# Attention with a first expert woven in: step schedule, relu engine, transposition copy and far factors changed

## The chip, the cores and the metric

The kernel runs on one core of a Trainium2 chip. The metric is the device time of one execution in microseconds (us). The kernel before took 723.59 us, the median of 3 runs (722.73 to 723.69).

## The reference

Attention over 4 batches, 8 heads, 768 positions and head size 64, and then a mixture of 8 experts over the 3072 tokens. A flag for each head, an input of the launch, says whether the head has the full causal mask or keeps only 4 sink positions and a window of 64.

```python
scores = scale * np.matmul(q, k.transpose(0, 1, 3, 2))
scores = np.where(mask[None, :, :, :], scores, -1000000000.0)
a = np.exp(scores - np.max(scores, axis=-1, keepdims=True))
attn = np.matmul(a / (np.sum(a, axis=-1, keepdims=True) + 1e-09), v)
x = attn.transpose(0, 2, 1, 3).reshape(B * S, H * D)          # 3072 x 512
P = np.exp(x @ w_gate - (x @ w_gate).max())
for _ in range(8):
    P /= P.sum(1, keepdims=True) + 1e-09
    P /= P.sum(0, keepdims=True) + 1e-09
    P *= N / E
for e in range(E):                                             # 8 experts, 512 -> 1024 -> 512
    out += P[:, e:e + 1] * (np.maximum(x @ w1[e], 0.0) @ w2[e])
```

## The kernel before

**Attention.** Batch b, a group g of 256 queries and a half u of the heads (4 heads, two pairs a) are a unit; there are 24. For each pair the keys come in chunks, g + 1 of them: 512 score columns, or 384 for the last one. A (unit, pair, chunk) is a task, and two tasks are a round: 48 rounds, 12 for each batch, of which 2 belong to g = 0, 4 to g = 1 and 6 to g = 2. In a round n, in the order of the code (lines 575 to 586): score matmuls (line 444) into PSUM; exp on ScalarE (453); masks on VectorE (462, 465); the preparation of a later unit, which transposes keys and queries on TensorE (248) into one PSUM tile `tr` and copies them on VectorE, keys first, then queries (255); the turn of a finished unit, four transpositions (312) and a copy on ScalarE into xT (315); the products with v for the round before (283), normalized on VectorE (296, 297); and then steps of expert 0.

Blocks of keys far from the diagonal need no mask tile: for them v is multiplied by a factor of 0 or 1 for each head (and 1 in the sink rows) ahead of time, `emit_vfar`, lines 260 to 267. The factors `farf` have one value for each head and block kind, and the multiplication reads them broadcast along the head's 66 columns.

**Expert 0** fills TensorE during attention. A query group of 256 tokens gives four layer-1 steps (two blocks of 128 hidden units, 8 matmuls of 256 columns, line 351, relu from PSUM at line 356 or 358) which count 1 unit each, and two layer-2 steps (8 matmuls of 512 columns, line 365, copy on ScalarE at 369), which count 2. That is 96 units in all. 72 are spent in the rounds by `spend`, and 24 are kept for the Sinkhorn part (line 605), whose iterations are a chain of small VectorE operations with one matmul (607) each. `late` chooses the relu's engine: VectorE in all rounds, ScalarE after them.

The tiles of `tr`, `xt`, the steps and the logits share two PSUM slots (tag "mo").

**Order.** Up to round 5 the order on TensorE, VectorE and ScalarE is the order of the code (`manual_schedule`). From round 6 on the framework's planner orders each engine by its own model of times, with the code's order as priority: the trace has steps of expert 0 some rounds ahead of their place in the code, and the far products of g = 2 (emitted in round 6) at 24.88 us, before round 4's scores.

**After attention** come the experts 1 to 7 with a fast matrix scheme (lines 636 to 858), which keeps TensorE full.

The quota before: from round 4 on, each round spends the rest of the 72 units over the rest of the rounds, rounded up. So rounds 4 to 31 emit 2 units each and rounds 32 to 47 one.

Of the kernel before, what the change touches and what calls it, by code (L numbers as in the profile page):

```python
# [16 lines left out]
ts = bass.ts  # L17
# [19 lines left out]
def kernel(  # L37
# [170 lines left out]
    sinks = [rows for rows in sinks if rows.stop > rows.start]  # L208
    masks = [cp.tile([128, 2, 640], F16, tag=f"mask{j}", name=f"mask{j}") for j in range(4)]
    farf = cp.tile([128, H, 2], F16, tag="farf")  # L210

    def make_keep():
        nc.vector.scalar_tensor_tensor(
            out=keep[:, 256:512], in0=wm, scalar=1.0, in1=fm, op0=ALU.add, op1=ALU.mult)
        nc.vector.tensor_copy(out=keep[:, 0:256], in_=keep[:, 256:512])
        for rows in sinks:
            nc.vector.tensor_scalar(out=keep[rows, 0:256], in0=fm[rows, :], scalar1=2.0,
                                    scalar2=None, op0=ALU.mult)
        nc.vector.tensor_copy(out=keep[:, 512:640], in_=keep[:, 256:384])

    def make_masks(js):
        for h in [2 * j + hh for j in js for hh in range(2)]:
# [18 lines left out]
    def emit_prep(b, g, u):  # L241

        tr = psA.tile([128, 512], F32, tag="mo", bufs=2, name=f"tr_{b}_{g}_{u}").bitcast(F16)
        for i, src in enumerate(kq[b, g]):
            for a in range(2):
                for c in range(2):
                    for hh in range(2):
                        nc.tensor.transpose(
                            out=tr[64 * hh:64 * hh + 64, ts(4 * i + 2 * a + c, 128)],
                            in_=src[:, 4 * u + 2 * a + hh, c, :], identity=ident16,  # L250
                        )
        kTs[b, g, u] = ap.tile([128, 2, 256], F16, tag=f"kT{u}{g}", name=f"kT_{b}_{g}_{u}")
        qTs[b, g, u] = ap.tile([128, 2, 256], F16, tag="qT", bufs=3, name=f"qT_{b}_{g}_{u}")
        for i, dst in enumerate((kTs[b, g, u], qTs[b, g, u])):
            nc.vector.tensor_copy(
                out=dst.rearrange("r a (n c p) -> r a c n p", c=2, p=64),
                in_=tr[:, ts(i, 512)].rearrange("r (a c n p) -> r a c n p", a=2, c=2, p=64),
            )

    def emit_vfar(b, g):  # L260
        if b not in vfs:
            vfs[b] = ap.tile([128, H, 4, DV], F16, tag="vf", bufs=1, name=f"vf_{b}")
        for n in (2 * g - 2, 2 * g - 1):
            nc.vector.tensor_tensor(
                out=vfs[b][:, :, n, :], in0=vts[b][:, :, n, :],
                in1=farf[:, :, min(n, 1)].unsqueeze(2).broadcast_to([128, H, DV]), op=ALU.mult,
            )

    def keep_warm(lhsT, src, n):
        for _ in range(n):  # L270
# [33 lines left out]
    def turn():  # L304

        while turns:
            b, g, u = turns.pop(0)
            xn = xns.pop((b, g, u))
            xt = psA.tile([128, 512], F32, tag="mo", bufs=2, name=f"xt_{b}_{g}_{u}").bitcast(F16)
            for a in range(2):  # L310
                for sb in range(2):
                    nc.tensor.transpose(out=xt[:, ts(2 * a + sb, 128)], in_=xn[:, a, sb],
                                        identity=ident16)
            c0 = b * S + 256 * g
            nc.scalar.activation(
                out=xT[u][:, :, c0:c0 + 256], in_=xt[:, 0:512].rearrange("p (a c) -> p a c", a=2),
                func=AF.Copy, bias=0.0, scale=1.0)
            if u == 1:
                one, two = first_steps(b, g)
                at = 4 if (b, g) == (0, 1) else len(fillers)  # L320
                fillers[at:at] = one
                fillers.extend(two)
# [94 lines left out]
    def emit_scores(i, a, ci):  # L417
        b, g, u = units[i]
        if a == 0 and ci == 0:
            if u == 0:  # L420
                nb, ng = divmod(3 * b + g + 3, 3)
                if g:
                    emit_vfar(b, g)
                if nb < B:
                    load_kq(nb, ng)
                    if ng == 1:
                        load_v_heads(nb, 0, 4)
                        load_v_heads(nb, 4, 8)
                elif ng == 0:
                    expw[1] = load_expert(1)  # L430
            if i + 1 < len(units):
                preps.append(units[i + 1])
        if ci == 0:
            PTs[i, a] = ap.tile([128, 2, PTW], F16, tag="PT", bufs=4, name=f"PT_{b}_{g}_{u}_{a}")
        PT = PTs[i, a]
        qT = qTs[b, g, u]
        chunk = chunks_of(g)[ci]
        sc = psA.tile([128, 2, 512], F32, tag="sc", bufs=2, name=f"sc_{i}_{a}_{ci}")
        width = sum(c[2] for c in chunk)
        off = 0  # L440
        for kj, qlo, L in chunk:
            for hh in range(2):
                r0 = 64 * hh
                nc.tensor.matmul(
                    out=sc[:, hh, off:off + L],
                    lhsT=kTs[b, kj // 2, u][r0:r0 + 64, a, ts(kj % 2, 128)],
                    rhs=qT[r0:r0 + 64, a, qlo:qlo + L], start=True, stop=True,
                )
            off += L
        c0 = 512 * ci  # L450

        def exp():
            nc.scalar.activation(
                out=PT[:, :, c0:c0 + width], in_=sc[:, :, 0:width],
                func=AF.Exp, bias=0.0, scale=SCALE,
            )

        def mask():
            m = masks[2 * u + a]
            if ci == g - 1:  # L460
                d = PT[:, :, c0 + 256:c0 + 384]
                nc.vector.tensor_tensor(out=d, in0=d, in1=m[:, :, 384:512], op=ALU.mult)
            if ci == g:
                d = PT[:, :, c0:c0 + 384]
                nc.vector.tensor_tensor(
                    out=d, in0=d, in1=m[:, :, 0:384] if g == 0 else m[:, :, 256:640],
                    op=ALU.mult)
        return exp, mask
# [4 lines left out]
    def fill(n):  # L473

        while n > 0 and fillers:
            done = fillers.pop(0)()
            n -= done
            left[0] -= done

    def finish_sums(hold=False):  # L480
        held = []
        for (i, a), (gen, scale) in list(sums_of.items()):
            while run(gen, 1):
                pass
            del sums_of[i, a]
            held += scale
        if not hold:
            for f in held:
                f()
        return held  # L490


    rounds = len(tasks) // 2
    quotas = [0] * 4 + [1] * (rounds - 4)

    def spend(n):
        if quotas[n]:
            fill(-(quotas[n] * (24 - left[0]) // sum(quotas[n:])))

    def sum_later(n):  # L500
        for i, a, ci in tasks[2 * n:2 * n + 2]:
# [19 lines left out]
    with tc.manual_schedule(engines=engines):  # L521
        keep_warm(blank[:, 0:128], blank, 9)
        make_far()
        make_keep()
        round_first(0)
        emit_prep(*units[0])
        round_first(4)
        r0 = scores(0)
        soften(r0, (0,))
        warm(3)  # L530
        make_masks((0, 1))
        emit_prep(*preps.pop())
        warm(2)
        place_v(0)
        r1 = scores(1)
        soften(r0, (1,))
        soften(r1, (0,))
        sum_later(0)
        warm(6)
        make_masks((2, 3))  # L540
        soften(r1, (1,))
        scale = finish_sums(True)
        emit_prep(*preps.pop())
        for f in scale:
            f()
        warm(4)
        sum_later(1)
        r2 = scores(2)
        soften(r2, (0,))
        turn()  # L550
        scale = finish_sums(True)
        soften(r2, (1,))
        for f in scale:
            f()
        sum_later(2)
        emit_prep(*preps.pop())
        warm(2)
        soften(scores(3))
        place_v(1)
        turn()  # L560
        finish_sums()
        sum_later(3)
        warm(2)
        soften(scores(4))
        turn()
        finish_sums()
        sum_later(4)
        spend(4)
        soften(scores(5))
        turn()  # L570
        finish_sums()
        sum_later(5)
        spend(5)
        emit_prep(*preps.pop())
    for n in range(6, rounds):
        soften(scores(n))
        if n == 7:
            place_v(2)
        if preps:
            emit_prep(*preps.pop())  # L580
        turn()
        finish_sums()
        sum_later(n)
        if n % 12 == 2 and n > 12:
            emit_logits(n // 12 - 1)
        spend(n)
# [307 lines left out]
```

The softmax here doesn't subtract the row's maximum and nothing guards it: scores larger than these inputs give would overflow.

## Time and profile before

| | |
|---|---|
| median of 3 runs | 723.59 us |
| the profiled execution | 722.74 us, its span 721.00 us |
| attention's first score matmul, round 6, first Sinkhorn reduction | 8.76, 34.05, 170.52 us |
| experts 1 to 7 begin on TensorE | 195.51 us |
| busy in the span | PE 693.6, weight loads 573.7, DVE 578.8, ACT 412.9, POOL 151.3 us |
| line 358, relu on VectorE | 36 of 0.68 us |
| line 356, relu on ScalarE | 12 of 0.60 us |
| line 255, copies of keys and queries | 48 of 0.42 us |
| line 264, far products | 16 of 0.69 us |

Engines: PE is TensorE, DVE VectorE, ACT ScalarE, POOL GpSimd. PE's busy time takes in its pipeline, so a busy PE is not one at its peak; the distances between the starts of matmuls tell more: 0.109 us for 256 columns and 0.216 us for 512 where nothing is in the way. A row of a table by stage has the stretch, its length, then busy time and number of instructions of each engine, the granted clock of TensorE as a share, the share of the DMA engines and GB/s. In a timeline a row has the start, the duration, engine, line, operation, tiles written and read, shapes, and in brackets the idle time of the engine before it and what ended that.

### The profile page before, as it was taken

The page shows a single profiled execution, that of the slowest core. Times are in us where ns is not written, and L with a number is a line of the kernel's source. Part 1 is how long each engine was busy: PE and PEld are TensorE (multiplying, and loading weights), DVE is VectorE, ACT ScalarE, POOL GpSimd, SP SyncE. Part 2 cuts the span into 40 slices and gives each one's busy share as a digit, 9 for nine tenths or more (in the row PEclk, how much of TensorE's full clock was granted, in tenths as well). Part 3 has the DMA queues.
Part 4 walks back from the last instruction along what each step waited for, and adds up shares of the span by engine and source line. Part 5 has one row for each costly group of instructions (what it writes and reads, how often), then busy time and mean ns, then how long its engine had stood idle before and what let it go on. Part 6 is the DMA issues. An engine that isn't in the chain of part 4 may idle for free.

```text
span 721.0 us, 17111 instructions
## 1 busy us (share of the span) xinstructions
PE 693.6 (96%) x6944; PEld 573.7 (80%) x6944; DVE 578.8 (80%) x1193; ACT 412.9 (57%) x770; POOL 151.3 (21%) x183
## 2 busy tenths in 40 slices
PE   7899999998999999999999999999999999999995
PEld 3566665665678888888888888888888888888884
DVE  7748675764789997888789888988888788887887
ACT  4675656674497555555555555555555555555550
POOL 6403040000002122212121222123121312121210
PEclk9999999998999999999999999999999999999999
DMA  9999394000344349434953395439642964245774
GB/s 179 179 171 104 31 92 42 2 2 2 54 79 74 54 70 165 85 56 74 153 91 65 63 147 101 75 60 145 104 75 48 146 107 80 48 79 109 148 156 126
DMA packets 84224, 65.62 MB, mean 91 GB/s; under 512 B 48304, under 2 KB 64688, under 8 KB 84144
## 3 DMA queue, kind: packets, MB, share of 16 engines
q0 software_dynamic: 74976, 57.17, 56.8%
q1 hardware_dynamic: 7536, 6.30, 3.7%
q8 instruction: 54, 0.88, 0.5%
q10 hardware_dynamic: 1632, 1.05, 0.5%
q14 instruction: 26, 0.21, 0.1%
HBM read 52.45 MB, written 6.29 MB: 81 GB/s over the span
## 4 chain that ended last, share of the span: by engine, by line
PE 68%; DVE 1%; issue 0%; ACT 0%; DVEq 0%
PE l1y L709 19%; PE l2y L778 19%; PE l2w L778 10%; PE l1w L709 10%; PE l2z L778 5%; PE l1z L709 5%; DVE acc_84 L795 1%; DVE S_7_5_10710 L646 0%; DVE S_7_5_10713 L646 0%; DVE S_7_5_10712 L646 0%; DVE acc_83 L795 0%; ACT R_3772 L718 0%; DVEq L889 0%; ACT add L792 0%; DVE S_7_5_10711 L646 0%
## 5 line engine op out<-in xcount | busy, mean ns | idle before, releaser
L792 ACT ACTIVATE add<-l2w,Pne 128x256 f32<-128x256 f32 x80 | 33.6, 473 | 66.1 <-PE l2w L778 64.2
L351 PEld LDWEIGHTS <-w_0_125 128*128 128x128 f16 x384 | 37.4, 102 | 8.7 <-issue 3.0
L792 ACT ACTIVATE add<-l2y,Pne 128x256 f32<-128x256 f32 x80 | 33.8, 474 | 10.9 <-PE l2y L778 10.2
L792 ACT ACTIVATE add<-l2z,Pne 128x256 f32<-128x256 f32 x80 | 33.6, 472 | 8.7 <-PE l2z L778 8.7
L800 POOL DMA_DIRECT2D acc_79<-add x21 | 17.7, 844 | 78.8 <-ACT add L792 57.7
L800 POOL DMA_DIRECT2D acc_82<-add x21 | 17.8, 847 | 68.0 <-ACT add L792 68.0
L800 POOL DMA_DIRECT2D acc_80<-add x21 | 17.7, 845 | 67.9 <-ACT add L792 67.9
L800 POOL DMA_DIRECT2D acc_81<-add x21 | 17.7, 844 | 68.0 <-ACT add L792 68.0
L800 POOL DMA_DIRECT2D acc_83<-add x18 | 15.1, 840 | 54.7 <-ACT add L792 46.8
L800 POOL DMA_DIRECT2D acc_84<-add x18 | 15.4, 854 | 44.2 <-ACT add L792 43.7
L795 DVE SCALAR_TENSOR_TENSOR acc_79<-l2y,Pne,acc_79 128x256 f32<-128x256 f32 x42 | 18.3, 476 | 7.2 <-PE l2y L778 7.1
L795 DVE SCALAR_TENSOR_TENSOR acc_83<-l2y,Pne,acc_83 128x256 f32<-128x256 f32 x44 | 19.1, 476 | 3.2 <-PE l2y L778 3.2
L795 DVE SCALAR_TENSOR_TENSOR acc_82<-l2y,Pne,acc_82 128x256 f32<-128x256 f32 x42 | 18.2, 476 | 4.1 <-PE l2y L778 4.1
L795 DVE SCALAR_TENSOR_TENSOR acc_80<-l2y,Pne,acc_80 128x256 f32<-128x256 f32 x42 | 18.2, 476 | 4.1 <-PE l2y L778 4.1
L795 DVE SCALAR_TENSOR_TENSOR acc_81<-l2y,Pne,acc_81 128x256 f32<-128x256 f32 x42 | 18.2, 475 | 4.1 <-PE l2y L778 4.1
L795 DVE SCALAR_TENSOR_TENSOR acc_84<-l2y,Pne,acc_84 128x256 f32<-128x256 f32 x36 | 15.6, 476 | 7.1 <-PE l2y L778 7.1
L709 PEld LDWEIGHTS <-S_2_3804 128*128 128x128 f16 x192 | 18.8, 98 | 2.4 <-issue 0.2
L709 PEld LDWEIGHTS <-S_7_9010 128*128 128x128 f16 x192 | 18.8, 98 | 2.2
L709 PEld LDWEIGHTS <-S_3_4874 128*128 128x128 f16 x192 | 18.8, 98 | 2.2
L709 PEld LDWEIGHTS <-S_4_5908 128*128 128x128 f16 x192 | 18.8, 98 | 2.2
L709 PEld LDWEIGHTS <-S_5_6942 128*128 128x128 f16 x192 | 18.8, 98 | 2.2
L709 PEld LDWEIGHTS <-S_6_7976 128*128 128x128 f16 x192 | 18.8, 98 | 2.2
(2597 smaller groups left out, 2279.1 us busy)
## 6 DMA issues: line engine op xcount, KB each, us to landing
acc_79<-add POOLq DMA_DIRECT2D x21, 256.0 KB, 3.5
acc_80<-add POOLq DMA_DIRECT2D x21, 256.0 KB, 3.3
acc_81<-add POOLq DMA_DIRECT2D x21, 256.0 KB, 3.3
acc_82<-add POOLq DMA_DIRECT2D x21, 256.0 KB, 3.3
acc_83<-add POOLq DMA_DIRECT2D x18, 256.0 KB, 3.6
acc_84<-add POOLq DMA_DIRECT2D x18, 256.0 KB, 10.0
w_0_125<-in_moe_w_dram POOLq DMA_DIRECT2D x1, 1024.0 KB, 11.4
w_0_132<-in_moe_w_dram POOLq DMA_DIRECT2D x1, 1024.0 KB, 18.4
```

What stands on the lines that cost most here:

```text
L351: nc.tensor.matmul(out=l1[:, ts(fb % 2, 256)], lhsT=w1[:, dc, ts(fb, 128)], rhs=xT[dc // 2][:, dc % 2, c0:c0 + 256], start=(dc == 0), stop ...
L709: nc.tensor.matmul(out=banks[g, bank][:, f, :], lhsT=lefts1[e][k - 1][:, dc, ts(2 * g + f, 128)], rhs=rights1[c][k - 1][:, dc, :], start=( ...
L778: nc.tensor.matmul(out=banks[bank][q], lhsT=lefts2[e, c][k - 1][:, q, f, :], rhs=rights2[e][k - 1][:, f, :], start=(first and (final or q ...
L792: nc.scalar.activation(out=t[:, q, :], in_=banks[bank][q], func=AF.Copy, bias=0.0, scale=w)
L795: nc.vector.scalar_tensor_tensor(out=dst, in0=banks[bank][q], scalar=w, in1=dst, op0=ALU.mult, op1=ALU.add,)
L800: nc.gpsimd.dma_start(out=acc[c][:, i, n, :, :], in_=t, accum_op=ALU.add)
```

## The change

Four things change together.

1. The 72 units of expert 0 start in round 6 and are spread evenly: after round n, 72 (n - 5) / 42 of them are due, rounded down. Rounds 4 and 5 spend none.
2. The relu of layer 1 is on ScalarE in rounds 12 to 17, 24 to 29 and 36 to 41 (g = 0 and 1 of batches 1 to 3), on VectorE in the other rounds.
3. One tile takes keys and queries, with one VectorE copy of 1024 columns instead of two of 512. The tile of groups 1 and 2 has one buffer, that of group 0 two.
4. The far factors are written out once, by three copies on ScalarE in round 2, to a tile with the factor in each column. A query group's two blocks are then one multiplication. The first of these moves from the start of round 2 to behind a preparation later in that round.

```diff
+    farx = cp.tile([128, H, 3, DV], F16, tag="farx")
...
+    def make_far_all():
+        for n in range(2):
+            nc.scalar.activation(
+                out=farx[:, :, n], in_=farf[:, :, n].unsqueeze(2).broadcast_to([128, H, DV]),
+                func=AF.Copy, bias=0.0, scale=1.0)
+        nc.scalar.activation(out=farx[:, :, 2], in_=farx[:, :, 1], func=AF.Copy, bias=0.0, scale=1.0)
...
-        kTs[b, g, u] = ap.tile([128, 2, 256], F16, tag=f"kT{u}{g}", name=f"kT_{b}_{g}_{u}")
-        qTs[b, g, u] = ap.tile([128, 2, 256], F16, tag="qT", bufs=3, name=f"qT_{b}_{g}_{u}")
-        for i, dst in enumerate((kTs[b, g, u], qTs[b, g, u])):
-            nc.vector.tensor_copy(
-                out=dst.rearrange("r a (n c p) -> r a c n p", c=2, p=64),
-                in_=tr[:, ts(i, 512)].rearrange("r (a c n p) -> r a c n p", a=2, c=2, p=64),
-            )
+        t = ap.tile([128, 2, 2, 256], F16, tag=f"kT{u}{g}", bufs=1 + (g == 0),
+                    name=f"kT_{b}_{g}_{u}")
+        kTs[b, g, u], qTs[b, g, u] = t[:, 0], t[:, 1]
+        nc.vector.tensor_copy(
+            out=t.rearrange("r i a (n c p) -> r (i a) c n p", c=2, p=64),
+            in_=tr.rearrange("r (i c n p) -> r i c n p", i=4, c=2, p=64),
+        )
...
-        for n in (2 * g - 2, 2 * g - 1):
-            nc.vector.tensor_tensor(
-                out=vfs[b][:, :, n, :], in0=vts[b][:, :, n, :],
-                in1=farf[:, :, min(n, 1)].unsqueeze(2).broadcast_to([128, H, DV]), op=ALU.mult,
-            )
+        n = 2 * g - 2
+        nc.vector.tensor_tensor(out=vfs[b][:, :, n:n + 2, :], in0=vts[b][:, :, n:n + 2, :],
+                                in1=farx[:, :, g - 1:g + 1, :], op=ALU.mult)
...
-                if g:
+                if g and (b, g) != (0, 1):
                     emit_vfar(b, g)
...
-    quotas = [0] * 4 + [1] * (rounds - 4)
+    weights = [0] * 6 + [1] * (rounds - 6)
 
     def spend(n):
-        if quotas[n]:
-            fill(-(quotas[n] * (24 - left[0]) // sum(quotas[n:])))
+        fill(left[0] - (96 - 72 * sum(weights[:n + 1]) // sum(weights)))
...
         turn()
+        make_far_all()
         scale = finish_sums(True)
...
         emit_prep(*preps.pop())
+        emit_vfar(0, 1)
         warm(2)
...
-        spend(4)
...
-        spend(5)
...
+        late[0] = n % 12 < 6
         turn()
```

## The prediction

> **What bounds the kernel now.** I read the page's slices first, then busy time by stage, then the timeline inside a stage with gaps, then the clock.
>
> ```profile
> PE   7899999998999999999999999999999999999995
> DVE  7748675764789997888789888988888788887887
> ACT  4675656674497555555555555555555555555550
> PEclk9999999998999999999999999999999999999999
> ```
>
> After slice 11 (18 us each, so from about 200 us) PE is at 9 to the end, and the chain that ended last lies 68% on PE, in lines 709 and 778. The diff doesn't touch those 525 us: they only start earlier or later. What can move is the stretch before them, cut here at rounds (a round is two tasks; its start is its first score matmul, line 444):
>
> ```profile
> core 0: us, PE busy (x) PEld busy (x) DVE busy (x) ACT busy (x) POOL busy (x), PEclk, DMA share, GB/s
> 25.69:34.05 8.36, 7.43 (x128) 6.39 (x128) 6.95 (x18) 3.94 (x5) 3.56 (x5) 1.00 2.15 171
> 34.05:52.29 18.24, 17.82 (x207) 10.77 (x207) 9.03 (x23) 14.04 (x18) 1.67 (x2) 1.00 1.61 184
> 52.29:72.77 20.48, 19.31 (x299) 13.66 (x298) 15.58 (x44) 12.79 (x19) 7.33 (x8) 1.00 1.20 93
> 72.77:93.67 20.90, 19.93 (x249) 12.98 (x248) 12.70 (x30) 13.43 (x18) 1.76 (x2) 1.00 0.27 27
> 93.67:115.26 21.59, 20.45 (x305) 13.98 (x305) 15.60 (x44) 13.27 (x20) 7.33 (x8) 1.00 1.41 87
> 115.26:133.92 18.66, 17.84 (x241) 12.21 (x242) 11.29 (x28) 13.24 (x18) 1.76 (x2) 1.00 0.29 30
> 133.92:153.24 19.32, 17.46 (x290) 12.11 (x290) 16.59 (x46) 13.05 (x20) 0.00 (x0) 1.00 0.01 3
> 153.24:170.07 16.83, 13.91 (x218) 8.90 (x218) 7.86 (x22) 12.91 (x17) 0.00 (x0) 0.96 0.01 2
> ```
>
> The rows are rounds 4-5, 6-11, 12-17 and so on to 42-47. PE leads everywhere, and DVE is heavy in every second row (query groups 0 and 1): 15.6 of 20.5 us. There PE stops, as at 98.9 us:
>
> ```profile
> 98.46 0.64 DVE L264 TENSOR_TENSOR vf_1894<-v_2_1100,farf 128x528 f16<-128x528 f16 x1
> 99.02 0.54 DVE L465 TENSOR_TENSOR PT_0_1_0_1806<-PT_0_1_0_1806,mask_108 128x768 f16<-128x768 f16 x1
> 99.15 0.62 ACT L315 ACTIVATE xT_77<-xt_2_1_1843 128x512 f16<-128x512 f16 x1
> 99.49 0.41 DVE L255 COPY kT_1_0_1839<-tr_1_0_1822 128x512 f16<-128x512 f16 x1
> 99.82 0.38 PE L351 MATMUL l_1874<-xT_76,w_0_125 128*128 128x256 f16 x2 [0.89 <-ACT xT_77 L315]
> ...
> 101.50 0.68 DVE L358 TENSOR_SCALAR hT_1_2_0_1849<-l_1874 128x512 f16<-128x512 f32 x1
> ...
> 102.15 1.02 ACT L453 ACTIVATE PT_1_0_0_1907<-sc_0_0_1908 128x1024 f16<-128x1024 f32 x1 [2.38 <-PE sc_0_0_1908 L444]
> ```
>
> A step of expert 0 waits for one of the two "mo" PSUM slots: one held by tr until the key and query copies, the other by xt until ACT's copy. DVE runs full from 97 to 100 us (3.00 of 3.00), while ACT idles 2.38 us before its next exp. The last finding is the clock:
>
> ```profile
> 165.26:168.67 3.41, 2.05 (x50) 1.63 (x46) 1.96 (x6) 1.83 (x3) 0.00 (x0) 1.00 0.00 0
> 168.67:172.08 3.41, 2.56 (x18) 1.74 (x19) 1.56 (x5) 0.88 (x3) 0.00 (x0) 0.50 0.00 0
> 172.08:175.49 3.41, 3.41 (x19) 2.54 (x18) 0.06 (x1) 1.19 (x3) 0.00 (x0) 0.50 0.02 5
> ```
>
> No step ran between 159.2 and 170.07 us; PE thinned out, and then worked 6.83 us at half clock.
>
> **What the Trainium skill says.** "VectorE: DVE Perf Modes", the perf-mode tier table: a tensor_tensor of 16-bit SBUF data runs two results a cycle, which needs step 1. The trace agrees: line 655 does 1024 elements in 0.68 us, while line 264, whose factor is a broadcast (step 0), takes 0.69 us for 528. The same page, TRN2 errata section: a PSUM source costs 120 + elements/2 cycles here, estimate 0.39 us for 512; line 255 shows 0.416. "ScalarE: Activation LUTs", Table sets: relu and copy are in every set, so a relu between exps needs no load; the trace has one load, at 1.31 us, and twelve relus on ACT after exps (line 356, 0.597 us each). "TensorE: Matmul & The Clock Gate", Part 1: after an idle window of about 3.4 us the clock halves until a busy one; the two windows above agree.
>
> **The change part by part.** Steps first. From the counts of lines 351 and 365 by stage (8 matmuls a step; line 365 counts two units) the units are 4, 12, 9, 13, 11, 11, 8, 4: 72. A unit streams 0.87 us on PE (8 x 0.109). New, from floor(72(n-5)/42): 0, 10, 10, 10, 11, 10, 10, 11. Below, "gaps" are the start-to-start excesses over 0.12 us between matmuls in the timeline, and "rest" is length - gaps - 0.87 x units, the attention work on PE:
>
> - rounds 6-11: gaps 0.9, rest 6.9; new need 6.9 + 8.7 = 15.6
> - 12-17: gaps 2.2, rest 10.5; 19.2
> - 18-23: gaps 1.6, rest 8.0; 16.7
> - 24-29: gaps 1.9, rest 10.1; 19.7
> - 30-35: gaps 1.3, rest 7.7; 16.4
> - 36-41: gaps 2.35, rest 10.0; 18.7
> - 42-47 to the Sinkhorn part: gaps 4.5, rest 8.8; 18.4
>
> Gaps now sum to 14.8; the new need without gaps is 124.7 us.
>
> DVE's relief: merged copy, 24 times: today 0.34 apart plus 0.41 = 0.75; new 120 + 512 cycles = 0.66 us as an estimate from the page, bounds 0.64 and 0.83 (two full copies); I take 0.66, so 0.1 less, 0.4 per six rounds. The score matmuls wait for both halves now too, so nothing gets later. Far product: 1056 packed elements by line 655, 0.70 us in place of 2 x 0.69; in rounds 12-17 two products, 1.4 us less; bounds 0.70 and 1.38. Relu: some 15 of 36 go from DVE (0.68) to ACT (0.60). So rounds 12-17: DVE 15.6 - 2.7 (4 relus) - 1.4 - 0.4 = 11.1; ACT 12.8 + 5 x 0.60 + 0.3 = 16.1 against PE's 19.2. In the other rows ACT stays near 13-14 against 16 or more. PE stays the bound, with DVE no longer near it.
>
> Added: three copies of 528 on ACT after round 2's xT copy, 0.60 each by line 315 (128x512), about 1.7 us. ACT ends that copy at 20.97 and idles 1.23 us until scores of round 3. So 0.3 to 0.6 us of delay for exp(3), place_v(1), and PV behind them; the first far product moves behind them on DVE and has 1 us to spare. If ACT's idle were not there, the full 1.7. I take 0.3.
>
> Rounds 4-5 without 4 units: then exp paces them (rounds 4 and 5 have 0.92 + 0.81 us each, after exp(4) starts at about 26.4), round 5's exps end near 29.9, masks at 30.5, key copy 31.6. Round 6's scores start at about 31.7 in place of 34.05: 2.35 us sooner, while the 4 units are paid later at 3.5. Alone a loss of 1.15 us; only filled gaps return it. Bounds: 0.9 to 3.5 sooner.
>
> Buffers: keys of groups 1 and 2 now have one buffer per u. The next batch's preparation comes two rounds or more after the last score that reads them; I cost that wait at nothing (cover about 5 us; a stall would cost up to one round, 3 us). No DMA is moved; GpSimd's loads are released by the same transposes.
>
> Gaps after: 10.0 (1.0, 1.3, 1.2, 1.3, 1.2, 1.4, 2.6). My reasons: round-boundary waits for xT copies stay (0.5 to 0.9 each, on ACT), DVE's part goes, and rounds 44-47, where PE waited on ACT for 0.25 to 0.54 us a round, get 8 units. The last exp, mask, PV, transposition, copy and logits are still serial. So Sinkhorn's first step starts at 31.7 + 124.7 + 10.0 = 166.4 in place of 170.07: 3.7 sooner.
>
> Clock: the 24 half-speed matmuls of line 351, which are 3 units, take 4.9 us in place of 2.6, and the first column sum comes at 174.96: 2.3 us lost. With 8 units in the last rounds the window before should be busy, but the serial end is 3 us long and the windows lie anywhere: I count 1.8 of 2.3.
>
> Sum: 3.7 + 1.8 = 5.5 us. The profiled execution took 722.74 (span 721.00 and 1.74 around it), so 717.2; the median is 0.85 higher, so **718.0**.
>
> **The rivals.**
> - Slower: ACT's queue. Relus stand between the exps in order; an exp waits until the step's matmuls end and its relu has run, then mask and PV wait. If each of the 15 relus is exposed with its 0.60 us, 9.0 us come in and use up the 5.5: 727. Against it: ACT is 16.1 of 19.2 and had 2.38 us idle before an exp. It decides where ACT's need passes PE's, or more than 9 of the relus are exposed.
> - The gaps don't close and the half clock returns: the waits named most are for xT copies on ACT, which stay. Then only 1 to 2 us: 722.
> - More: DVE was the cause of most gaps. Gaps 7, clock fully kept, opening at its best: 9 us, 714.
> - Nothing: the planner reorders rounds 6-47 anyhow (six rounds emit 6 units there, yet the trace shows 8 in 36-41 and 4 in 42-47). Then it evens out as before: 723.6.
>
> **Chances.** Main case (716 to 720.5) 0.52; more 0.15; little 0.13, half of it inside 0.2%; nothing 0.08; slower 0.12. 0.2% (1.4 us) is about what a measurement of this kernel can tell from no change. Faster: 0.52 + 0.15 + 0.07 = 0.74; same 0.06 + 0.08 = 0.14; slower 0.12. The range 713 to 723.6 leaves out the slower case and the edge of the best one.
>
> **What would show it.** Right: round 6 near 31.7; stages with 10 or 11 units; line 264's successor at 0.70 us; the merged copy at 0.66; DVE near 11 us in rounds 12-17; first Sinkhorn reduction near 167; clock 1.00 there. Wrong: PE waits in rounds 12-17, 24-29 and 36-41 that name a relu or an exp on ACT; a half-clock window in 25-32 us, which lost 3.4 us of matmuls; a wait of tr's copy for an old key buffer.

## The result, and the profile after

The changed kernel takes 720.71 us, the median of 4 runs (719.37 to 720.98); the kernel before took 723.64 beside it (722.73 to 725.43). The ratio is 0.9953, 95% interval 0.993 to 0.9976: 2.9 us faster by the medians, where 5.5 were forecast. (The ratio is worked out from all the runs; it is not the quotient of the two medians, 0.9960.) The profiled execution took 719.37 us with a span of 717.7, against 722.74 and 721.0.

The page's slices of the changed kernel:

```profile
PE   7799999999999999999999999999999999999996
DVE  6665465755779997888788888988898788887887
ACT  4767777685596555555555555555555555555550
PEclk9999999999999999999999999999999999999999
```

VectorE lost load in most of the first ten slices and ScalarE took some; the dip of PE in the tenth slice (162 to 180 us) is gone. By stage, with the columns of the table in the prediction (rounds 4-5, 6-11 and so on; the last row ends where the last logits begin):

```profile
26.21:32.12 5.91, 5.20 (x87) 3.60 (x87) 3.73 (x11) 3.94 (x5) 2.58 (x3) 0.72 2.00 173
32.12:50.32 18.20, 17.25 (x223) 11.66 (x223) 10.85 (x25) 12.96 (x16) 2.64 (x3) 1.00 1.73 186
50.32:70.72 20.40, 18.62 (x290) 12.36 (x290) 13.11 (x37) 14.22 (x22) 7.34 (x8) 1.00 1.52 107
70.72:89.11 18.39, 18.17 (x234) 11.52 (x234) 8.47 (x20) 13.96 (x20) 1.75 (x2) 1.00 0.31 30
89.11:110.67 21.56, 20.14 (x308) 13.84 (x306) 12.76 (x37) 15.42 (x24) 7.33 (x8) 1.00 1.23 87
110.67:128.90 18.23, 17.50 (x234) 11.51 (x234) 9.99 (x25) 13.82 (x19) 1.75 (x2) 1.00 0.30 31
128.90:150.63 21.73, 20.33 (x306) 13.98 (x306) 13.89 (x36) 15.63 (x24) 0.00 (x0) 1.00 0.01 2
150.63:169.48 18.85, 17.78 (x254) 11.70 (x253) 8.98 (x23) 14.32 (x19) 0.00 (x0) 1.00 0.01 2
```

Round 6 starts at 32.12 in place of 34.05 us, 1.93 sooner. Rounds 12-17 and 24-29 hold 9 and 11 units in both kernels, and they are as long as they were (20.40 and 21.56 against 20.48 and 21.59) although VectorE has about 2.5 to 2.8 us less to do in them. From round 6 to the first Sinkhorn reduction it is now 137.94 us, before 136.47, with four more units in it. So attention as a whole ends 0.46 us sooner: putting off the four units was nearly neutral by itself. The rest of the gain comes right after it. First the changed kernel, its first reduction and first column sum, then the kernel before's column sum (its first reduction was at 170.52):

```profile
170.06 0.35 DVE L603 TENSOR_REDUCE rs<-Pne 128x24 f32<-128x192 f32 x1 [1.62 <-ACT Pne L342]
...
172.26 0.29 PE L613 MATMUL cs_3234<-bs,ones_95 128*128 128x8 f32 x2
```

```profile
175.17 0.43 PE L607 MATMUL cs_3286<-bs,ones_95 128*128 128x8 f32 x2
```

2.20 us in place of 4.65: the steps that stand ahead of the column sum on PE run at full clock. The half clock of 168.67 to 175.49 us is gone, but another one has come, in rounds 4 and 5 (the clock is the third column from the end; the last two rows are the end of attention):

```profile
22.66:26.07 3.41, 1.68 (x24) 0.94 (x23) 2.38 (x6) 3.15 (x5) 1.84 (x2) 1.00 1.26 210
26.07:29.48 3.41, 3.33 (x33) 1.76 (x32) 1.64 (x6) 2.60 (x3) 0.08 (x1) 0.50 1.77 182
166.02:169.43 3.41, 2.64 (x50) 1.82 (x47) 1.56 (x5) 1.54 (x3) 0.00 (x0) 1.00 0.00 0
169.43:172.84 3.41, 3.36 (x37) 3.05 (x38) 1.74 (x6) 1.79 (x4) 0.00 (x0) 1.00 0.00 0
```

Experts 1 to 7 begin on PE at 192.45 us instead of 195.51 and take the same 525 us from there. The profiles differ by 3.3 us: 0.46 in attention, 2.45 to the first column sum, 0.15 in the rest of the Sinkhorn part and 0.28 in the experts. Single profiles scatter by about as much: of three kernels with the same code up to round 6 (the kernel before, tail_warm of experiment 3 and before_copy_first of experiment 7) one starts round 6 at 34.05 us, one at 36.29 and one at 35.19; and from the first column sum to the end, where the code is the same in all, the profiles of this document take 545.3 to 547.4 us. So the profiles show where time goes, and the medians what a change is worth.

And the gaps stayed, but for the last stage (4.5 before, 1.7 now). Round 25 of the changed kernel, where the kernel before stopped for 1.05 us (some rows left out):

```profile
93.46 0.81 ACT L459 ACTIVATE PT_0_1_0_1718<-sc_0_0_1719 128x768 f16<-128x768 f32 x1
93.54 0.39 PE L256 MATMUL tr_1_0_1734<-ident_93,q_2_1_1050 128*64 128x128 f16 x8
93.86 0.40 PE L318 MATMUL xt_2_1_1753<-ident_93,xn_2_1_1639 128*128 128x128 f16 x4
94.28 0.34 PE L289 MATMUL pv_0_0_1_1771<-v_2_1053,PT_0_0_1_1653 128*128 128x65 f16 x6
94.30 0.56 DVE L471 TENSOR_TENSOR PT_0_1_0_1718<-PT_0_1_0_1718,mask_108 128x768 f16<-128x768 f16 x1 [0.65 <-ACT PT_0_1_0_1718 L459]
94.77 0.69 DVE L263 COPY kT_1_0_1751<-tr_1_0_1734 128x1024 f16<-128x1024 f16 x1
94.84 0.62 ACT L321 ACTIVATE xT_77<-xt_2_1_1753 128x512 f16<-128x512 f16 x1
95.51 0.38 PE L357 MATMUL l_1784<-xT_76,w_0_126 128*128 128x256 f16 x2 [0.88 <-ACT xT_77 L321]
```

PE stops for 1.05 us again, with VectorE idle for 0.65 us just before. The transpositions into tr are done at 93.93, yet their copy stands behind a mask whose exp ends at 94.27. So both "mo" slots, tr's and xt's, come free at 95.46, together. The wait is named for ScalarE's copy; the other slot is as late.

In the kernel before, the stop in round 25 had another cause. There the step went on at 99.82 us, when xT's copy had ended (99.77), while the copy of the queries out of tr had not even begun:

```profile
100.29 0.41 DVE L255 COPY qT_1_0_1840<-tr_1_0_1822 128x512 f16<-128x512 f16 x1
```

So this step did not wait for tr's slot. The named wait, for xT's copy on ScalarE, was the one that counted, and VectorE's load was not what held it.

### The profile page after: what moved, and what is told of

The parts are those of the page before. It is cut to its first block, busy times and chain, and to the rows that moved or that the text cites. A ratio compares the mean times of both kernels' runs of the same rounds, so it can differ in the third digit from the quotient of the medians.

```text
span 717.7 us, 17079 instructions
## 1 busy us (share of the span) xinstructions
PE 692.1 (96%) x6944; PEld 571.5 (80%) x6944; DVE 563.7 (79%) x1147; ACT 422.5 (59%) x787; POOL 151.5 (21%) x183
## 3 DMA queue, kind: packets, MB, share of 16 engines
q10 hardware_dynamic: 1632, 1.05, 0.5%
## 4 chain that ended last, share of the span: by engine, by line
PE 67%; DVE 2%; issue 0%; ACT 0%; DVEq 0%
PE l1y L715 19%; PE l2y L784 19%; PE l2w L784 10%; PE l1w L715 10%; PE l2z L784 5%; PE l1z L715 5%; DVE acc_84 L801 1%; DVE acc_83 L801 0%; DVE hT_5_4259 L730 0%; DVE S_1_4_4253 L652 0%; DVE S_7_5_10658 L652 0%; ACT hT_4_4077 L754 0%; DVE S_7_5_10661 L652 0%; DVE T_2_4115 L661 0%; DVE S_7_5_10660 L652 0%
## 5 line engine op out<-in xcount | busy, mean ns | idle before, releaser
L357 PEld LDWEIGHTS <-w_0_126 128*128 128x128 f16 x384 | 35.8, 98 | 6.9 <-issue 2.9
L715 PEld LDWEIGHTS <-S_5_6890 128*128 128x128 f16 x192 | 18.8, 98 | 2.2
L715 PEld LDWEIGHTS <-S_3_4822 128*128 128x128 f16 x192 | 18.8, 98 | 2.2
L715 PEld LDWEIGHTS <-S_4_5856 128*128 128x128 f16 x192 | 18.8, 98 | 2.2
L715 PEld LDWEIGHTS <-S_7_8958 128*128 128x128 f16 x192 | 18.8, 98 | 2.2
L715 PEld LDWEIGHTS <-S_6_7924 128*128 128x128 f16 x192 | 18.8, 98 | 2.2
L715 PEld LDWEIGHTS <-S_2_3752 128*128 128x128 f16 x192 | 18.8, 98 | 2.2
```

Of the source, the lines that this page charges most:

```text
L357: nc.tensor.matmul(out=l1[:, ts(fb % 2, 256)], lhsT=w1[:, dc, ts(fb, 128)], rhs=xT[dc // 2][:, dc % 2, c0:c0 + 256], start=(dc == 0), stop ...
L715: nc.tensor.matmul(out=banks[g, bank][:, f, :], lhsT=lefts1[e][k - 1][:, dc, ts(2 * g + f, 128)], rhs=rights1[c][k - 1][:, dc, :], start=( ...
```

## The experiments

Theory A: the gain is the clock at the end of attention, kept up by the steps that the even spread leaves for rounds 44 to 47; inside attention PE's own work and the boundary waits set the time. Theory B is the prediction's: VectorE's relief and the spread close gaps. "Gaps" are measured as in the prediction (14.8 us before in rounds 6 to 47, 11.9 in the changed kernel). The stretch from round 6 to the first Sinkhorn reduction took 136.5 us before and 137.9 in the changed kernel. Every ratio is to the kernel before on the same chip.

**1. The spread alone.**

```diff
 # kernel before, with
-    quotas = [0] * 4 + [1] * (rounds - 4)
+    weights = [0] * 6 + [1] * (rounds - 6)
...
-        if quotas[n]:
-            fill(-(quotas[n] * (24 - left[0]) // sum(quotas[n:])))
+        fill(left[0] - (96 - 72 * sum(weights[:n + 1]) // sum(weights)))
...
-        spend(4)
...
-        spend(5)
```

> The kernel before with only the even spread of the steps (rounds 4 and 5 spend none); relu, copies and far products as before. Theory A (most of the 3 us is the half clock at the end of attention, kept away because steps are left for rounds 44 to 47): 720.5 to 721.7, clock 1.00 around the first Sinkhorn iteration, first column sum within 2.5 us of the first reduction. Theory B (VectorE's relief is what lets the steps fit): 722.8 to 724.5, with gaps back in rounds 12-17, 24-29 and 36-41.

721.16 us, ratio 0.9978 (0.9971 to 0.9985); first column sum 2.19 us after the reduction. Rounds 6 to the reduction take 138.2 us, 0.3 more than with everything, and the gaps are 11.6, as with everything: VectorE's relief closed none of them. The spread alone brings the larger part of the gain, 2.1 of the 2.9 us by the medians (1.6 of 3.4 by the ratios, whose intervals overlap).

**2. Everything but the spread.**

```diff
 # changed kernel, with
-    weights = [0] * 6 + [1] * (rounds - 6)
+    quotas = [0] * 4 + [1] * (rounds - 4)
...
-        fill(left[0] - (96 - 72 * sum(weights[:n + 1]) // sum(weights)))
+        if quotas[n]:
+            fill(-(quotas[n] * (24 - left[0]) // sum(quotas[n:])))
...
+        spend(4)
...
+        spend(5)
```

> The changed kernel with the quota of before (2 units from round 4, 1 from round 32); relu on ScalarE, the merged copy and the written-out factors stay. Theory A: the rounds 44 to 47 are empty again and the half clock comes back: 722.3 to 723.6. Theory B: the relief of VectorE holds the gain: 720.3 to 721.5.

724.97 us, ratio 1.0021 (1.0011 to 1.0032): slower than before. The half clock at the end is back, and the reduction and column sum stand 4.65 us apart:

```profile
172.22 0.35 DVE L606 TENSOR_REDUCE rs<-Pne 128x24 f32<-128x192 f32 x1 [1.74 <-ACT Pne L342]
...
176.87 0.34 PE L616 MATMUL cs<-bs,ones 128*128 128x8 f32 x2
```

This is worse than expected. In its profile another half clock covers the four steps of rounds 4 and 5:

```profile
26.80:30.20 3.40, 3.40 (x32) 2.46 (x32) 1.66 (x6) 1.73 (x2) 1.07 (x2) 0.50 1.90 176
```

Rounds 4 and 5 take 9.71 us here and 8.36 in the profile of the kernel before, at full clock; with no steps in them they take 5.6 to 6.1 in every profile of the even spread, with half clock or without. There was also more half clock over all: five of these 14 runs have a mean clock of 0.982 to 0.984, and none of the 56 of the kernel before is under 0.988. From round 6 to the reduction it takes 135.7 us, 0.8 less than the kernel before, with gaps of 14.3: that is all that VectorE's relief and the moved relus give with the old quota. Theory B falls as the main cause.

**3. The clock alone.**

```diff
 # kernel before, with
+    keep_warm(xT[0][:, 0, NTOK - 128:NTOK], xT[0][:, 0, NTOK - 512:NTOK], 8)
     finish_sums()
     turn()
     emit_logits(B - 1)
```

> The kernel before with 8 extra matmuls of 512 columns (results unused) just before the last products with v, and nothing else. Theory A: the clock stays full, the first Sinkhorn iteration is 2.2 us shorter, and the extra matmuls lie in waiting time: 721.2 to 722.2. Theory B: the end was bound by the serial chain and not by the clock, so the extra matmuls cost up to their 1.7 us: 723.5 to 725.3.

722.30 us, ratio 0.9988 (0.998 to 0.9995), a little above what theory A gave. In its profile the extra matmuls fill a wait for the last masks, and the column sum follows the reduction by 2.19 us:

```profile
167.75 1.90 PE L272 MATMUL warm<-xT 128*128 128x512 f16 x8
...
172.62 0.35 DVE L598 TENSOR_REDUCE rs<-Pne 128x24 f32<-128x192 f32 x1 [1.62 <-ACT Pne L336]
...
174.81 0.29 PE L608 MATMUL cs<-bs,ones 128*128 128x8 f32 x2
```

So theory A's mechanism is there, without any of the change. In the median it is worth 1.0 us and not 2.2. The 56 runs of the kernel before in this group differ in their mean clock: 18 of them with 0.995 have a median of 722.26 us, 12 with 0.988 one of 723.46. It may be that not every execution has both half-clock windows at the end, but this is not shown: four runs with 0.996 or 0.997 took 723.0 to 723.9 us, and the profile of before_copy_first (experiment 7) has both windows at a mean clock of 0.994. A second part of the spread's gain may be that it takes the steps out of rounds 4 and 5, where half clock made them dear in experiment 2; that was not tested alone.

**4. The relu's engine**, all on VectorE, and then all on ScalarE.

```diff
-        late[0] = n % 12 < 6
```

> The changed kernel with every relu of the rounds on VectorE. Theory A: the relu's engine does nothing, 720.2 to 721.4. Theory B: the relief of VectorE in rounds 12-17, 24-29 and 36-41 matters, 722 to 724. A third way: relus on ScalarE had cost something, 718.5 to 720.

720.68 us, ratio 0.9969 (0.9957 to 0.9981), rounds 6 to the reduction 137.4 us: not to be told from the changed kernel.

```diff
-        late[0] = n % 12 < 6
+        late[0] = True
```

> The changed kernel with all 36 relus of the rounds on ScalarE. Theory A (the relu's engine doesn't set the time): 720.2 to 721.5. Theory B, the prediction's slower rival with its cost doubled (relus delay the exps in ScalarE's queue): 0.3 to 0.6 us for each of the 22 more, a part of them exposed, 723.5 to 728.

722.03 us, ratio 0.9984 (0.9974 to 0.9994); rounds 6 to the reduction 138.7 us, 0.8 more than the changed kernel for 22 more relus on ScalarE, 0.04 us each. The time is a little above what theory A gave, and below the slower rival's. Part of it may be the clock: the 22 runs go from 720.4 (clock 0.993) to 724.6 (0.985).

**5. xT's copy on VectorE.**

```diff
-            nc.scalar.activation(
-                out=xT[u][:, :, c0:c0 + 256], in_=xt[:, 0:512].rearrange("p (a c) -> p a c", a=2),
-                func=AF.Copy, bias=0.0, scale=1.0)
+            nc.vector.tensor_copy(
+                out=xT[u][:, :, c0:c0 + 256], in_=xt[:, 0:512].rearrange("p (a c) -> p a c", a=2))
```

> The changed kernel, with the copies of transposed attention outputs to xT (24 of 128x512) on VectorE instead of ScalarE. Theory A (the gaps that stayed are PSUM slots held by xt until ScalarE has done the two exps ahead of the copy, so neither the steps' spread nor VectorE's relief could close them): the three gaps of 1.05 us at rounds 13, 25 and 37 shrink to 0.4 or less, gaps of rounds 6 to 47 fall from 11.9 to 7-9 us, time 717.5 to 719.7. Rival (the boundary wait is set by something else of the same round, the preparation's copy or the exps themselves): gaps within 1 us of the changed kernel's, 720.2 to 721.5.

718.98 us, ratio 0.9943 (0.9931 to 0.9955). The time is what was expected, the reason isn't: the gap in round 25 is still 1.05 us, now with "DVE kT" as the releaser, and gaps fall only to 11.0 us. From round 6 to the reduction it takes 2.0 us less than the changed kernel; the other 1.1 us of that isn't in gaps over 0.12 us, and where it lies was not settled. So the copy on ScalarE alone did not make the wait.

**6. The spread from round 4, and extra matmuls in the opening.**

```diff
-    weights = [0] * 6 + [1] * (rounds - 6)
+    weights = [0] * 4 + [1] * (rounds - 4)
...
+        spend(4)
...
+        spend(5)
```

> The changed kernel with the even spread begun in round 4 (3 units in rounds 4 and 5, the rest evenly). Theory A (putting off the 4 units of rounds 4 and 5 gains 1.9 us there and costs them again later): round 6 starts 1 to 1.7 us later than in the changed kernel, rounds 6 to 47 are 2 to 2.6 us shorter, 719.5 to 720.5. Rival (the early start is itself worth what it gains): 721 to 722.5.

721.57 us, ratio 0.9978 (0.997 to 0.9987). In its profile half clock lies over 24.8 to 31.6 us, and round 6 starts at 37.0; from there 136.2 us, 1.7 less than the changed kernel, with three units fewer. The time is no better than the changed kernel's, and it is the rival's. Of the 4.9 us by which round 6 is later, 1.9 stand there when round 4 starts, ahead of the steps, so this profile doesn't price them.

```diff
         soften(scores(3))
+        warm(5)
         place_v(1)
```

> The changed kernel with 5 extra matmuls of 512 columns (results unused) in the wait ahead of the second placement of v, in round 3. Theory A (the half-clock window at 26.1 us comes from that wait and costs about 0.4 us): no half clock between 22 and 33 us, round 6 0.2 to 0.5 us sooner, 720.0 to 720.7. Rival (the opening is paced by exp, and half clock there costs nothing): within 0.2 of the changed kernel, or up to 0.5 later where the extra matmuls delay v.

721.10 us, ratio 0.997 (0.996 to 0.9981). There is no half clock in the opening of its profile, but round 6 starts at 32.7, not sooner. It is not to be told from the changed kernel.

**7. The copy of keys and queries ahead of the masks.** The planner had put it behind a mask in round 25. An order edge changes that (`emit_prep` returns its copy, and what stands in the block of `issue_after` is queued behind it):

```diff
-        soften(scores(n))
+        r = scores(n)
+        soften(r, (0,))
...
-            emit_prep(*preps.pop())
+            with tc.issue_after(emit_prep(*preps.pop()).ins):
+                soften(r, (1,))
+        else:
+            soften(r, (1,))
```

> The changed kernel, where from round 6 on VectorE's copy of the transposed keys and queries is queued ahead of the same round's masks instead of between or behind them. Theory A' (the three gaps of 1.05 us at rounds 13, 25 and 37 are a PSUM slot held because the copy stands behind a mask that still waits for its exp, not because VectorE is short of time): these gaps fall to about 0.3, the sum of gaps from 11.9 to about 9.5, time 718.4 to 719.6. Rival (the later masks hold back the products with v by as much): 720.2 to 721.6.

718.36 us, ratio 0.9944 (0.9926 to 0.9962), gaps 9.5. Round 25 in its profile:

```profile
93.12 0.69 DVE L263 COPY kT<-tr 128x1024 f16<-128x1024 f16 x1 [0.19 <-PE tr L256]
93.25 0.53 PE L289 MATMUL pv<-v,PT 128*128 128x65 f16 x12
93.73 1.01 DVE L471 TENSOR_TENSOR PT<-PT,mask 128x768 f16<-128x768 f16 x2
93.87 1.80 PE L357 MATMUL l<-xT,w 128*128 128x256 f16 x15
93.99 0.62 ACT L321 ACTIVATE xT<-xt 128x512 f16<-128x512 f16 x1
```

The copy starts with the transpositions' end, the step starts when the copy ends, and xT's copy comes later without harm. The three stops of 1.05 us, in rounds 13, 25 and 37, fall to 0.26 each. That in the changed kernel they were VectorE's order is shown. The interval of this ratio overlaps that of the changed kernel, but the profiled executions of the two have the same half-clock windows before the experts, and from round 6 to the reduction this one takes 135.7 us, 2.3 less. The same edge on the kernel before, and then both edits of 5 and 7, without and with the five matmuls of 6:

> The kernel before, with nothing but its copies of keys and queries queued ahead of the same round's masks from round 6 on. If the gaps that the change left are a matter of VectorE's order alone, independent of the steps' spread and of the relief: gaps of the rounds 12-17, 24-29 and 36-41 fall by 1.5 to 2.5 us together, time 1.3 to 2.5 us below the kernel before, 721 to 722. If the order pays only once VectorE has been relieved: within 0.7 us of the kernel before.

722.14 us, ratio 0.9982 (0.9972 to 0.9992); gaps of rounds 12-17, 24-29 and 36-41 fall from 6.4 to 4.8. The order pays without the relief too, with 1.3 us of the medians. But it does not close every gap: in round 25 of this kernel the stop is still 1.05 us, and here the named wait is the right one. The copies out of tr end at 99.92 us, xT's copy on ScalarE ends at 100.25, and the step starts then:

```profile
99.50 0.42 DVE L255 COPY qT<-tr 128x512 f16<-128x512 f16 x1
99.63 0.62 ACT L316 ACTIVATE xT<-xt 128x512 f16<-128x512 f16 x1
100.30 1.47 PE L352 MATMUL l<-xT,w 128*128 128x256 f16 x12 [0.88 <-ACT xT L316]
```

> copy_first with xT's copies on VectorE as well. If the two waits are separate, the gains add: 716.6 to 718.0, gaps near 8.5. If both are the same slot's wait, no more than the better of the two: 718.4 to 719.2.

715.41 us, ratio 0.9895 (0.9877 to 0.9914), gaps 7.3: the gains add, and the time is 1.2 us below the best that was expected.

> copy_first_xt with 5 extra matmuls ahead of the second placement of v. If half clock in rounds 3 to 5 costs what the profiles show (0.2 to 0.5 us in the median, more in single runs): 0.2 to 0.6 below copy_first_xt and a narrower spread. If not: within 0.2 of it.

714.23 us, ratio 0.988 (0.9862 to 0.9898), round 6 at 31.5 us. That is 1.2 us below the run without the matmuls, more than was expected, and not for the reason given: that one's profile has no half clock in the opening either. Round 6 starts 0.5 sooner; 5 and 4 runs can't settle why. It is the fastest of the kernels run, 8.8 us by the medians below the kernel before.

## Why the prediction was right or wrong

- **The direction and the range** held; the size did not: 2.9 us where 5.5 stood (the profiles give 3.3). 720.7 lies just outside the main case of 716 to 720.5, in the one called little. That the total came as near as this is partly luck: the larger term, 3.7 us from attention itself, came out at 0.46, and the smaller one, the clock, above its count. Of the 3.2 us that attention lacks, 1.9 are gaps, 0.4 the opening and 0.9 PE's need.
- **The clock**: 1.8 of 2.3 us counted, 2.45 measured between the profiles. The mechanism was right, and it is the largest part of what the profiles differ by. Experiments 1 and 2 show that the gain needs the spread and not the relief, and experiment 3 that the clock can be kept without either. There it gave 1.0 us in the medians, less than half of the gain; what else the spread's 2.1 us are made of is open. One reading was wrong: the window at 165.26 us, which was taken to agree with an idle window, had PE busy for 2.05 of 3.41 us.
- **The opening**: round 6 was put at 31.7, it came at 32.12. The half-clock window in 25-32 us, listed as something that would show the prediction wrong, came about; exp of round 3 started 0.5 us later (0.3 counted), and PE's wait behind it grew from 1.11 to 1.51 us.
- **The step that failed** is "Gaps after: 10.0", with "round-boundary waits for xT copies stay ... DVE's part goes". They are 11.9: 2.6 in rounds 12-17 (1.3 said), 1.9 in 24-29 and in 36-41 (1.3 and 1.4). The profile of before had been read as a lack of VectorE time. Its own example, round 25, was a wait for xT's copy; and in the changed kernel, where VectorE idles before the copy, the wait is a place in VectorE's queue: the copy waits behind a mask that waits for an exp. Taking load off VectorE closed neither. Elsewhere it went both ways: 1.6 in rounds 6-11 (1.0 said) and 1.5 in 30-35 (1.2), but 0.7 in 18-23 (1.2) and 1.7 in the last stage (2.6).
- **PE's need** was put at 124.7 us without gaps. The steps after attention start at 169.64 us, so it was 169.64 - 32.12 - 11.9 = 125.6. What the 0.9 us more are was not found.
- **The terms of VectorE** were right: merged copy 0.68 to 0.69 us (0.66 said), far product 0.65 to 0.71 (0.70), three copies on ScalarE 0.64 to 0.65 (0.60). Only 14 relus moved in the trace, 15 said. VectorE came to 13.1 us in rounds 12-17, where 11.1 stood; only two of their four relus moved. The relief had little to buy: VectorE's busy time fell by 15 us, and rounds 12-17 and 24-29 stayed as long. The old key buffer, costed at nothing, cost nothing: before line 263 VectorE waits for transpositions alone.
- **The slower rival** (relus in ScalarE's queue) fell: 22 more of them cost 0.8 us in the profile. **"Nothing"** fell by experiment 1. The rival "gaps don't close and the half clock returns" was half right: the gaps didn't, the clock did not fall.

Open: what the 1.1 us of experiment 5 outside gaps is, how often each half-clock window occurs, and how the spread's gain divides between the end of attention and its opening.

## What to carry to other kernels

Load taken off an engine bought nothing here where the waits came from the order of its queue, or from another engine's: see what stands ahead of the instruction that frees the buffer, and whether that one waits itself. The engine named by a wait on a shared pair of buffers is the one that came last; look at when the other came free, since either can be the one that counts. And filler work was worth most where TensorE had thinned out before a dense stretch: it filled the waits there, and it paid again in the clock afterwards.

## What the runs showed of the hardware that was not expected

Half clock came without an idle window: after 3.41 us in which PE was busy for 1.68 (22.66 to 26.07 in the changed kernel) or 2.05 us (165.26 to 168.67 before), but not after 2.64 (166.02 to 169.43). PE's busy time alone doesn't decide it: in the kernel before, the clock stayed full after a window with 1.82 us, and in experiment 2's profile it fell after one with 2.27 (the first and the second line; both windows are in step with the half-clock ones of their profile).

```profile
21.89:25.30 3.41, 1.82 (x31) 1.23 (x28) 2.22 (x6) 3.10 (x4) 2.47 (x3) 1.00 1.30 207
166.74:170.15 3.41, 2.27 (x50) 1.73 (x49) 1.73 (x6) 2.06 (x3) 0.00 (x0) 1.00 0.00 0
```

What else counts was not found. "TensorE: Matmul & The Clock Gate" in the Trainium skill speaks in Part 1 of an idle window; these were not idle. The mean granted clock of runs of one kernel goes from 0.988 to 0.997 (the 56 runs of the kernel before in experiment 3) with times from 721.8 to 725.4 us, but the highest clock does not go with the lowest time.
